# Sums of the seven-product keys read per pair of PSUM banks, and one summed form of x split early

## The chip, the cores and the metric

The kernel runs on one core of one Trainium2 chip. Its metric is the device time of one execution in microseconds (us). Before the change the median of three runs is 595.16 us (593.99 to 596.32). The engines are PE (matrix products), DVE (vector), ACT (scalar functions), POOL and SP, whose queue issues the DMAs. SBUF is the memory on the chip, PSUM the banks that PE writes its products to; DVE and ACT read them from there.

## The reference

Two stages, all in float32. Batch 8, 8 heads of 64, sequence 576, model width 512, inner width 1024.

```
p_packed = softmax(p k^T / 8) v            # 32 packed rows a head
x        = softmax(q p_packed^T / 8) p_packed
x        = heads side by side, 8 x 576 rows of 512
x_prev   = x moved by one row (zeros first)
xk = mu_k x + (1 - mu_k) x_prev ;  xr = mu_r x + (1 - mu_r) x_prev
out = sigmoid(xr w_r) * ( relu(xk w_k)^2 w_v )
```

## The kernel before

The 8 x 576 = 4608 rows of x are worked in nine blocks of 512 rows. Each block needs its gates (`xr w_r`), its keys (`xk w_k`, then relu and square), and its values (the squares times `w_v`, times the gates). Every operand of these products is held as two float32r parts, a high one and a low one, and a product is three matmuls: high by high, high by low, low by high. So one 128 x 128 by 128 x 512 product is three matmuls.

The last two blocks (`PAIR`, called first and second here) have their keys computed together. Rows and columns are taken as a 2 x 2 arrangement: the two blocks of xk by its two halves of width (a, b for the first block and c, d for the second), and `w_k` by its halves of rows and columns. Seven products instead of eight give the four results; this is Strassen's scheme in Winograd's form. `quarters` builds the row side: A11 is a, A12 is b, S3 = a - c, S2 = d - S3, S1 = a + S2, S4 = b - S2, A22 is d. `sums_of_w` builds the sums of `w_k` (T1 to T4) earlier. Each row form is split into a high and a low part on DVE (`parted_form`: a cast at L1419 and a subtraction at L1421), two row blocks u a form, and the parts lie in two tiles (`form_tiles`), one buffer each, taken from the four `xt` buffers.

`keys_of_pair` then runs the seven passes in the order A11, A12, S2, S3, S1, A22, S4. A pass goes over four column blocks j, and for each over two row blocks u, with three matmuls (L1551 to L1553), 24 in all. Four passes go into Z, four PSUM banks of one tile each (`m`, shown as `ph`): A11 leaves P1 there, S2 adds to it (U2), S3 adds again (U3), A22 again. After A11, S2 and S3, ACT copies each bank to SBUF (`kept`, L1471), and only then may the next pass add to that bank. Three passes go into X: A12, S1 and S4. X is four banks that lie in pairs in two PSUM tiles (`twin`, shown as `pa`), j = 0 and 1 in the first, 2 and 3 in the second. Behind these, `made_of` adds the bank to the copy of P1, U3 or U2 on DVE (L1484), and ACT takes relu and square in place (L1489, L1491). The results lie in SBUF tiles `q`, two column blocks a tile, in eight `sq` buffers; `home` takes two for each of the four results. A pass gives its two form buffers back when its last matmul is issued:

```
for slot, _ in forms[name]:
    flow.give("xt", slot)
```

`parted_square` splits a square into two parts for the value product (L1508, L1510). Its buffers come from `xk`, freed as the forms S3, S1, A22 and S4 are made, and from `xt`, freed after the passes. The value product of a block goes over eight blocks f of squares (L1250 to L1252), f = 0 to 3 from the first column half, 4 to 7 from the second.

The order of the work is not written out by hand. A planner (`Flow`) runs all these generators with an estimated cost for each instruction (`vec`, `act`, `pe`), picks the one that could start first by its estimate, and issues the instructions in that order; each engine then takes its own in that order. `take` and `give` hand out buffers, `wait` and `set` are events; both order the plan. The waits that the chip makes come from the tiles that the instructions read and write: who comes later in the order waits for who came earlier on the same tile.

Of the kernel before, what the change touches and what calls it, by code (L numbers as in the profile page):

```python
# [9 lines left out]
F32R = mybir.dt.float32r  # L10
# [163 lines left out]
def attn_pack_channel_mix(ctx: ExitStack, tc: tile.TileContext, q, k, v, p, mu_k, mu_r, w_k, w_v, w_r, out):  # L174
# [1200 lines left out]
    def quarters():  # L1375

        yield from mix(PAIR[0], 2, xrs, "xr")
        yield from mix(PAIR[1], 2, xrs, "xr")
        flow.now.rank = 1.1
        A, slots = {}, {}  # L1380
        for i in PAIR:
            for h in range(2):
                slots[i, h] = yield from flow.take("xk")
                A[i, h] = tile_([P, HC, TB], F32, "xk", slots[i, h], "xq")
            yield from mixed_whole(i, 0, [A[i, c // HC][:, c % HC, :] for c in range(NC)])
        (a, b), (c, d) = ((A[i, 0], A[i, 1]) for i in PAIR)
        (sa, sb_), (sc, sd) = ((slots[i, 0], slots[i, 1]) for i in PAIR)
        yield from formed("A11", a)
        yield from formed("A12", b)
        forms["S2"] = yield from form_tiles()  # L1390
        for u in range(HC):
            yield vec(TB)
            nc.vector.tensor_tensor(c[:, u, :], a[:, u, :], c[:, u, :], op=ALU.subtract)
            st_ = yield from flow.take("tmp")
            s2 = tile_([P, TB], F32, "tmp", st_, "s2")
            yield vec(TB)
            nc.vector.tensor_tensor(s2, d[:, u, :], c[:, u, :], op=ALU.subtract)
            yield from parted_form("S2", s2, u)
            yield vec(TB)
            nc.vector.tensor_tensor(a[:, u, :], a[:, u, :], s2, op=ALU.add)  # L1400
            yield vec(TB)
            nc.vector.tensor_tensor(b[:, u, :], b[:, u, :], s2, op=ALU.subtract)
            flow.give("tmp", st_)
        for name, x, slot in (("S3", c, sc), ("S1", a, sa), ("A22", d, sd), ("S4", b, sb_)):
            yield from formed(name, x)
            flow.give("xk", slot)

    def form_tiles():
        got = []
        for part in range(2):  # L1410
            slot = yield from flow.take("xt")
            o = LEAD["xt"][slot]
            got.append((slot, tile_([P, 2 * (S + 1)], F32R, "xt", slot, "form")[:, o:o + HC * TB].rearrange("p (u t) -> p u t", u=HC)))
        return got

    def parted_form(name, x, u):
        (_, h), (_, l) = forms[name]
        yield vec2(TB)
        nc.vector.tensor_copy(h[:, u, :], x)  # L1419
        yield vec(TB)  # L1420
        nc.vector.tensor_tensor(l[:, u, :], x, h[:, u, :].bitcast(F32), op=ALU.subtract)  # L1421
        flow.set((name, u))
# [24 lines left out]

    def keys_of_pair():

        ms, pas = [], []  # L1450
        for j in range(HF):
            ms.append((yield from flow.take("m")))
        Z = [ps.tile([P, TB], F32, name="ph", tag=f"m{slot}") for slot in ms]
        pas = yield from two_slots()
        twin = [banks(slot) for slot in pas]
        X = [twin[j // 2][:, j % 2, :] for j in range(HF)]
        Q = {}

        def home(i, h):
            for g in range(HF // 2):  # L1460
                slot = yield from flow.take("sq")
                Q[i, h, g] = slot, tile_([P, 2, TB], F32, "sq", slot, "q")
            flow.set(("home", i, h))

        def rest(i, h, j):
            return Q[i, h, j // 2][1][:, j % 2, :]

        def kept(n, j, i, h):
            yield from flow.wait(("home", i, h))
            yield act(TB)  # L1470
            nc.scalar.copy(rest(i, h, j), Z[j])  # L1471
            flow.set(("kept", n, j))

        def made_of(bank, j, i, h, n):
            yield from flow.wait(("home", i, h))
            to = rest(i, h, j)
            if n is None:
                yield act(TB)
                nc.scalar.activation(to, bank[j], AF.Relu)
                flow.give("m", ms[j])  # L1480
            else:
                yield from flow.wait(("kept", n, j))
                yield vec(TB)
                nc.vector.tensor_tensor(to, bank[j], to, op=ALU.add)  # L1484
                flow.set(("read", i, h, j))
                if (i, h) == (PAIR[0], 1) and j % 2:
                    flow.give("pa", pas[j // 2])
                yield act(TB)
                nc.scalar.activation(to, to, AF.Relu)  # L1489
            yield act(TB)  # L1490
            nc.scalar.activation(to, to, AF.Square)  # L1491
            flow.set(("r", i, HF * h + j))

        def squares():
            for i in PAIR:
                for f in range(NF):
                    yield from flow.wait(("r", i, f))
                    tag = "xk" if f < HF else "xt"
                    slot = yield from flow.take(tag)
                    o = LEAD[tag][slot] if tag == "xt" else 0  # L1500
                    size = 2 * (S + 1) if tag == "xt" else 2 * TB
                    hl = tile_([P, size], F32R, tag, slot, "hl")[:, o:o + 2 * TB].rearrange("p (u t) -> p u t", u=2)
                    flow.spawn(parted_square(i, f, slot, hl), 0)

        def parted_square(i, f, slot, hl):
            raw = rest(i, f // HF, f % HF)
            yield vec2(TB)
            nc.vector.tensor_copy(hl[:, 0, :], raw)  # L1508
            yield vec(TB)
            nc.vector.tensor_tensor(hl[:, 1, :], raw, hl[:, 0, :].bitcast(F32), op=ALU.subtract)  # L1510
            sqs[i, f] = slot, hl
            flow.set(("sq", i, f))

        flow.spawn(squares(), 0.5)
        first, second = PAIR
        for h in range(2):
            flow.spawn(home(first, h), 0)
            flow.spawn(home(second, 1 - h), 0)

        def own(c, o):  # L1520
            return [(wk_h[:, c + u, o:o + WP], wk_l[:, c + u, o:o + WP]) for u in range(HC)], ()

        def summed(name):
            return None, [(name, u) for u in range(HC)]

        passes = (
            ("A11", own(0, 0), Z, True, None, lambda j: kept("P1", j, first, 0)),
            ("A12", own(HC, 0), X, True, None, lambda j: made_of(X, j, first, 0, "P1")),
            ("S2", summed(T2), Z, False, "P1", lambda j: kept("U2", j, first, 1)),
            ("S3", summed(T3), Z, False, "U2", lambda j: kept("U3", j, second, 1)),  # L1530
            ("S1", summed(T1), X, True, (first, 0), lambda j: made_of(X, j, second, 1, "U3")),
            ("A22", summed(T4), Z, False, "U3", lambda j: made_of(Z, j, second, 0, None)),
            ("S4", own(HC, WP), X, False, (second, 1), lambda j: made_of(X, j, first, 1, "U2")),
        )
        for n, (name, (ws, events), bank, opens, before, evict) in enumerate(passes):
            yield from flow.wait(*events)
            if ws is None:
                ws = [small[events[u]] for u in range(HC)]
            for j in range(HF):
                if isinstance(before, str):  # L1540
                    yield from flow.wait(("kept", before, j))
                elif before:
                    yield from flow.wait(("read", *before, j))
                js = slice(j * P, (j + 1) * P)
                for u in range(HC):
                    yield from flow.wait((name, u))
                    (_, xh), (_, xl) = forms[name]
                    yield pe(0.685)
                    flow.now.t -= flow.LAG
                    wh, wl = ws[u][0][:, js], ws[u][1][:, js]  # L1550
                    nc.tensor.matmul(bank[j], wh, xh[:, u, :], start=(opens and u == 0), stop=False, skip_group_check=(not opens))  # L1551
                    nc.tensor.matmul(bank[j], wh, xl[:, u, :], start=False, stop=False, skip_group_check=(not opens))  # L1552
                    nc.tensor.matmul(bank[j], wl, xh[:, u, :], start=False, stop=(u == HC - 1), skip_group_check=(not opens))  # L1553
                flow.spawn(evict(j), 0, flow.t + flow.LAG)
            for slot, _ in forms[name]:
                flow.give("xt", slot)

    def fronts():
        for b in range(B):
# [94 lines left out]
```

## Time and profile before

| | us | share of the span |
|---|---|---|
| profiled execution | 595.77 | |
| its span, first to last instruction | 593.6 | |
| PE busy | 576.8 | 97% |
| DVE busy | 407.7 | 69% |
| ACT busy | 321.1 | 54% |
| median of three runs | 595.16 | |

The mean granted clock of TensorE over the span is 0.997 of full speed. Busy time is the time in which an engine had an instruction under way. The chain of waits follows the work back from the last instruction, and says whose work set the end. The passes of the pair run between 497.6 and 546.1 us of the span, the value products of both blocks after them.

### The profile page before, as it was taken

To read this page: it belongs to the slowest core of one execution; us is meant where nothing else is said; L and a number is where in the kernel's file an instruction comes from. 1 tells how busy PE (TensorE), PEld (TensorE's weight loads), DVE (VectorE), ACT (ScalarE), POOL (GpSimd) and SP (SyncE) were. 2 spreads that over 40 slices of the span, in tenths; PEclk is the share of its full clock that TensorE was granted. 3 is DMA by queue.
4 is the path that set the end of the run, shared out by engine and by line. 5 is a ranking of instruction groups with operands and counts; after the bars stand their busy time and mean duration, and the time that the engine had idled before them with its cause. 6 is when DMAs were issued, how large, how long until landed. Compare 5 with 4: busy or idle time off the path is not lost.

```text
span 593.6 us, 10565 instructions
## 1 busy us (share of the span) xinstructions
PE 576.8 (97%) x4091; PEld 451.6 (76%) x4091; DVE 407.7 (69%) x766; ACT 321.1 (54%) x581; POOL 7.8 (1%) x33
## 2 busy tenths in 40 slices
PE   7999999999999999999999999999999999788997
PEld 6877777687777778777877777777788888566885
DVE  1999799857792997198738877659865564766421
ACT  5679974755743682377347745547555553447000
POOL 3000000000000000000000000000000000000000
PEclk9999999999999999999999999999999999899999
DMA  8897331863466365327613755710100010000011
GB/s 301 332 258 218 106 62 20 192 135 51 111 136 142 78 114 129 85 39 142 145 72 71 155 101 152 157 25 0 72 1 0 1 72 1 0 1 1 0 72 71
DMA packets 160594, 56.67 MB, mean 95 GB/s; under 512 B 136856, under 2 KB 150304, under 8 KB 160544
## 3 DMA queue, kind: packets, MB, share of 16 engines
q1 hardware_dynamic: 160224, 55.86, 37.4%
q8 instruction: 32, 0.52, 0.4%
q0 software_dynamic: 320, 0.14, 0.1%
q14 instruction: 18, 0.15, 0.1%
HBM read 43.00 MB, written 12.98 MB: 94 GB/s over the span
## 4 chain that ended last, share of the span: by engine, by line
PE 73%; DVE 16%; DMA 4%; ACT 3%; issue 2%; SPq 1%; DVEq 0%; ACTq 0%
PE pvo L1250 8%; PE pvo L1251 8%; PE pvo L1252 8%; PE ph L1162 8%; PE ph L1163 7%; PE ph L1164 7%; PE pr L1211 5%; PE pr L1213 5%; PE pr L1212 5%; DVE x L1117 2%; PE pa L706 2%; DMA st<-in_moe_w_r 1%; PE ph L1552 1%; PE ph L1553 1%; PE ph L1551 1%
## 5 line engine op out<-in xcount | busy, mean ns | idle before, releaser
L1162 PE MATMUL ph<-xk,wk_h 128*128 128x512 f32 x224 | 90.7, 405 | 0.0
L1250 PE MATMUL pvo<-wv,sq 128*128 128x512 f32 x224 | 89.0, 397 | 0.0
L1163 PE MATMUL ph<-xk,wk_h 128*128 128x512 f32 x224 | 87.5, 391 | 0.0
L1164 PE MATMUL ph<-xk,wk_l 128*128 128x512 f32 x224 | 87.3, 390 | 0.0
L1251 PE MATMUL pvo<-wv,sq 128*128 128x512 f32 x224 | 87.3, 390 | 0.0
L1252 PE MATMUL pvo<-wv,sq 128*128 128x512 f32 x224 | 87.2, 389 | 0.0
L1174 ACT ACTIVATE r<-ph 128x512 f32<-128x512 f32 x56 | 33.6, 601 | 52.2 <-PE ph L1164 50.2
L1211 PE MATMUL pr<-wr_h,xr 128*128 128x512 f32 x144 | 57.8, 401 | 0.9 <-ACT xr L1137 0.7
L1213 PE MATMUL pr<-wr_h,xr 128*128 128x512 f32 x144 | 56.3, 391 | 0.8 <-DVE xr L1139 0.8
L1212 PE MATMUL pr<-wr_l,xr 128*128 128x512 f32 x144 | 56.2, 390 | 0.0
L1162 PEld LDWEIGHTS ph<-xk,wk_h 128*128 128x128 f32 x224 | 42.0, 188 | 14.3 <-issue 5.9
L1250 PEld LDWEIGHTS pvo<-wv,sq 128*128 128x128 f32 x224 | 42.1, 188 | 13.6 <-issue 4.9
L1117 DVE SCALAR_TENSOR_TENSOR x<-xt,mus,x 128x128 f32<-128x128 f32 (+6 forms) x100 | 46.5, 504 | 4.7 <-ACT x L1111 4.5
L1252 PEld LDWEIGHTS pvo<-wv,sq 128*128 128x128 f32 x224 | 42.0, 188 | 9.0
L1164 PEld LDWEIGHTS ph<-xk,wk_l 128*128 128x128 f32 x224 | 42.0, 188 | 9.0
L1251 PEld LDWEIGHTS pvo<-wv,sq 128*128 128x128 f32 x224 | 42.1, 188 | 8.1
L1111 ACT ACTIVATE x<-xt,mus 128x128 f32<-128x128 f32 (+6 forms) x100 | 47.6, 522 | 1.2 <-DVE sq L1187 1.2
L1163 PEld LDWEIGHTS ph<-xk,wk_h 128*128 128x128 f32 x224 | 42.1, 188 | 7.6 <-DVE xk L1056 0.2
L1185 DVE CAST sq<-r 128x512 fp32r<-128x512 f32 x48 | 20.1, 418 | 34.2 <-ACT r L1177 33.5
L1187 DVE TENSOR_TENSOR sq<-r,sq 128x512 fp32r<-128x512 f32 x56 | 38.0, 679 | 4.1 <-ACT sq L1182 3.3
L1072 ACT COPY xt<-pa 128x576 f32<-128x576 f32 x28 | 30.6, 1173 | 10.8 <-PE pa L898 10.7
L1177 ACT ACTIVATE r<-r 128x512 f32<-128x512 f32 x56 | 35.5, 634 | 1.2
(205 smaller groups left out, 977.9 us busy)
## 6 DMA issues: line engine op xcount, KB each, us to landing
vt<-in_v SPq DMA_DIRECT2D x14, 512.0 KB, 4.6
raw<-in_k SPq DMA_DIRECT2D x96, 72.0 KB, 2.7
raw<-in_q SPq DMA_DIRECT2D x96, 72.0 KB, 2.7
out<-sig SPq DMA_DIRECT2D x27, 256.0 KB, 3.0
st<-in_moe_w_k SPq DMA_DIRECT2D x8, 512.0 KB, 9.9
st<-in_moe_w_v SPq DMA_DIRECT2D x8, 512.0 KB, 4.7
far<-at SPq DMA_DIRECT2D x12, 288.0 KB, 2.5
aTd<-far SPq DMA_DIRECT2D x12, 256.0 KB, 3.0
```

Source lines behind the costliest of these rows:

```text
L1111: nc.scalar.mul(x32[:, o:o + n], xts[b, c][:, 1 + s:1 + s + n], mus[:, j, c:c + 1])
L1117: nc.vector.scalar_tensor_tensor(x32[:, o:o + n], xts[b, c][:, s:s + n], mus[:, j + 1, c:c + 1], x32[:, o:o + n], op0=ALU.mult, op1=ALU.add,)
L1162: nc.tensor.matmul(ph, wk_h[:, c, fs], xh, start=(c == 0), stop=False)
L1163: nc.tensor.matmul(ph, wk_h[:, c, fs], xl, start=False, stop=False)
L1164: nc.tensor.matmul(ph, wk_l[:, c, fs], xh, start=False, stop=(c == NC - 1))
L1187: nc.vector.tensor_tensor(hl[:, 1, :], r, hl[:, 0, :].bitcast(F32), op=ALU.subtract)
L1211: nc.tensor.matmul(pr, xh[:, ts_], wr_h[:, c, :], start=(c == 0), stop=False)
L1212: nc.tensor.matmul(pr, xh[:, ts_], wr_l[:, c, :], start=False, stop=False)
L1213: nc.tensor.matmul(pr, xl[:, ts_], wr_h[:, c, :], start=False, stop=(c == NC - 1))
L1250: nc.tensor.matmul(pv[t], sh, wvs[f][:, 0, :], start=(f == 0), stop=False)
L1251: nc.tensor.matmul(pv[t], sh, wvs[f][:, 1, :], start=False, stop=False)
L1252: nc.tensor.matmul(pv[t], sl, wvs[f][:, 0, :], start=False, stop=(f == NF - 1))
```

## The change

It does two things in the keys of the pair.

First, `made_of` is replaced by `added` and `last_of_four`. `added` does nothing after an even j. After an odd j it adds the whole pair, both banks of the tile, to the whole tile `q` in one instruction of 1024 elements, and relu and square also run over 1024. `last_of_four` is the former case of A22, which reads a Z bank alone and is as before.

Second, the tiles of the form S2 are taken from two `sq` buffers in place of two `xt` buffers. A form now carries the tag of its buffers, and they are given back to that tag behind the pass. The other six forms take `xt` buffers as before.

```diff
         yield from formed("A11", a)
         yield from formed("A12", b)
-        forms["S2"] = yield from form_tiles()
+        early = []
+        for part in range(2):
+            slot = yield from flow.take("sq")
+            early.append(("sq", slot, tile_([P, HC, TB], F32R, "sq", slot, "form")))
+        forms["S2"] = early
...
-        def made_of(bank, j, i, h, n):
-            yield from flow.wait(("home", i, h))
-            to = rest(i, h, j)
-            if n is None:
-                yield act(TB)
-                nc.scalar.activation(to, bank[j], AF.Relu)
-                flow.give("m", ms[j])
-            else:
-                yield from flow.wait(("kept", n, j))
-                yield vec(TB)
-                nc.vector.tensor_tensor(to, bank[j], to, op=ALU.add)
-                flow.set(("read", i, h, j))
-                if (i, h) == (PAIR[0], 1) and j % 2:
-                    flow.give("pa", pas[j // 2])
-                yield act(TB)
-                nc.scalar.activation(to, to, AF.Relu)
+        def last_of_four(j):
+            yield from flow.wait(("home", second, 0))
+            to = rest(second, 0, j)
+            yield act(TB)
+            nc.scalar.activation(to, Z[j], AF.Relu)
+            flow.give("m", ms[j])
             yield act(TB)
             nc.scalar.activation(to, to, AF.Square)
+            flow.set(("r", second, j))
+
+        def added(j, i, h, n):
+            if not j % 2:
+                return
+            yield from flow.wait(("home", i, h), ("kept", n, j - 1), ("kept", n, j))
+            to = Q[i, h, j // 2][1]
+            yield vec(2 * TB)
+            nc.vector.tensor_tensor(to, twin[j // 2], to, op=ALU.add)
+            flow.set(("read", i, h, j - 1))
+            flow.set(("read", i, h, j))
+            if (i, h) == (first, 1):
+                flow.give("pa", pas[j // 2])
+            yield act(2 * TB)
+            nc.scalar.activation(to, to, AF.Relu)
+            yield act(2 * TB)
+            nc.scalar.activation(to, to, AF.Square)
+            flow.set(("r", i, HF * h + j - 1))
             flow.set(("r", i, HF * h + j))
...
-            ("A12", own(HC, 0), X, True, None, lambda j: made_of(X, j, first, 0, "P1")),
+            ("A12", own(HC, 0), X, True, None, lambda j: added(j, first, 0, "P1")),
...
-            for slot, _ in forms[name]:
-                flow.give("xt", slot)
+            for tag, slot, _ in forms[name]:
+                flow.give(tag, slot)
```

## Rows read from the trace of the kernel before

**Rows 1.** The page: busy time of the engines; the chain that ended last, by engine.

```profile
PE 576.8 (97%) x4091; PEld 451.6 (76%) x4091; DVE 407.7 (69%) x766; ACT 321.1 (54%) x581; POOL 7.8 (1%) x33
...
PE 73%; DVE 16%; DMA 4%; ACT 3%; issue 2%; SPq 1%; DVEq 0%; ACTq 0%
```

**Rows 2.** Waits, 497.5 to 546.1: waiter, releaser, total us, times, longest us.

```profile
DVE form L1419 <- PE ph L1553: 9.9, 3, 6.0
...
PE pa L1551 <- DVE q L1484: 4.1, 5, 0.9
...
PE ph L1551 <- DVE form L1419: 2.4, 1, 2.4
```

**Rows 3.** Windows: stretch, length, busy PE PEld DVE ACT POOL, granted clock, DMA, GB/s.

```profile
497.58:503.02 5.44, 5.44 (x26) 4.50 (x24) 0.00 (x0) 2.36 (x4) 0.00 (x0) 1.00 0.01 3
503.02:509.60 6.58, 5.73 (x25) 4.42 (x24) 3.61 (x6) 3.12 (x5) 0.00 (x0) 1.00 0.00 0
...
514.70:517.70 3.00, 3.00 (x8) 2.34 (x7) 2.80 (x7) 0.85 (x2) 0.00 (x0) 0.50 0.00 0
...
525.32:533.05 7.73, 6.02 (x26) 4.35 (x25) 5.15 (x9) 3.92 (x7) 0.00 (x0) 1.00 0.00 1
533.05:538.50 5.45, 5.45 (x26) 4.50 (x24) 3.77 (x7) 4.60 (x9) 0.00 (x0) 1.00 0.00 0
538.50:546.09 7.59, 6.03 (x26) 4.35 (x25) 3.93 (x7) 4.75 (x9) 0.00 (x0) 1.00 0.01 2
546.09:589.80 43.71, 43.71 (x193) 35.85 (x191) 16.00 (x29) 1.73 (x3) 0.00 (x0) 1.00 0.08 29
```

**Rows 4.** Timeline of PE in A12 and S2: start, us, engine, line [idle before].

```profile
504.15 0.39 PE L1553 MATMUL pa<-form,wk_l 128*128 128x512 f32 x1
...
504.83 0.39 PE L1553 MATMUL pa<-form,wk_l 128*128 128x512 f32 x1
506.07 0.50 PE L1551 MATMUL pa<-form,wk_h 128*128 128x512 f32 x1 [0.85 <-DVE q L1484]
...
507.56 0.39 PE L1551 MATMUL pa<-form,wk_h 128*128 128x512 f32 x1
...
510.06 0.39 PE L1553 MATMUL ph<-form,T 128*128 128x512 f32 x1
512.88 0.49 PE L1551 MATMUL ph<-form,T 128*128 128x512 f32 x1 [2.43 <-DVE form L1419]
```

**Rows 5.** Timeline of DVE, 495 to 513 us.

```profile
495.78 0.68 DVE L1393 TENSOR_TENSOR xq<-xq 128x512 f32<-128x512 f32 x1
...
503.22 0.43 DVE L1419 CAST form<-s 128x512 fp32r<-128x512 f32 x1 [6.02 <-PE ph L1553]
505.32 0.69 DVE L1484 TENSOR_TENSOR q<-pa,q 128x512 f32<-128x512 f32 x1 [1.68 <-PE pa L1553]
...
507.14 0.69 DVE L1484 TENSOR_TENSOR q<-pa,q 128x512 f32<-128x512 f32 x1 [0.53 <-PE pa L1553]
...
509.87 0.69 DVE L1484 TENSOR_TENSOR q<-pa,q 128x512 f32<-128x512 f32 x1 [0.84 <-PE pa L1553]
...
512.86 0.69 DVE L1421 TENSOR_TENSOR form<-s,form 128x512 fp32r<-128x512 f32 x1
```

**Rows 6.** Groups by line: tile, out<-in, count, busy us, mean ns, idle before.

```profile
L1484 DVE TENSOR_TENSOR q<-pa,q 128x512 f32<-128x512 f32 x12 | 8.3, 690 | 9.5 <-PE pa L1553 8.6 <-ACT q L1491 0.8
...
L1489 ACT ACTIVATE q<-q 128x512 f32<-128x512 f32 x12 | 7.6, 632 | 11.7 <-DVE q L1484 11.7
L1471 ACT COPY q<-ph 128x512 f32<-128x512 f32 x12 | 7.0, 587 | 11.4 <-PE ph L1553 11.4
...
L738 ACT COPY ppT<-pa 128x128 f32<-128x128 f32 x7 | 1.9, 265 | 11.2 <-PE pa L735 11.2
...
L996 DVE TENSOR_TENSOR pms<-pm,mub 128x128 f32<-128x128 f32 x2 | 0.6, 284 | 0.0
```

**Rows 7.** Timeline of ACT: the last gate of the pair's first block.

```profile
486.90 0.60 ACT L1231 ACTIVATE sig<-pr 128x512 f32<-128x512 f32 x1 [1.28 <-PE pr L1213]
```

More of the change, by code (lines that the diff above doesn't have):

```diff
@@ L1412, in form_tiles @@
             o = LEAD["xt"][slot]
-            got.append((slot, tile_([P, 2 * (S + 1)], F32R, "xt", slot, "form")[:, o:o + HC * TB].rearrange("p (u t) -> p u t", u=HC)))
+            got.append(("xt", slot, tile_([P, 2 * (S + 1)], F32R, "xt", slot, "form")[:, o:o + HC * TB].rearrange("p (u t) -> p u t", u=HC)))
         return got
     def parted_form(name, x, u):
-        (_, h), (_, l) = forms[name]
+        (*_, h), (*_, l) = forms[name]
         yield vec2(TB)
@@ L1448, in keys_of_pair @@
     def keys_of_pair():
+        first, second = PAIR
         ms, pas = [], []
@@ L1514, in keys_of_pair @@
         flow.spawn(squares(), 0.5)
-        first, second = PAIR
         for h in range(2):
@@ L1527, in keys_of_pair @@
             ("A11", own(0, 0), Z, True, None, lambda j: kept("P1", j, first, 0)),
-            ("A12", own(HC, 0), X, True, None, lambda j: made_of(X, j, first, 0, "P1")),
+            ("A12", own(HC, 0), X, True, None, lambda j: added(j, first, 0, "P1")),
             ("S2", summed(T2), Z, False, "P1", lambda j: kept("U2", j, first, 1)),
             ("S3", summed(T3), Z, False, "U2", lambda j: kept("U3", j, second, 1)),
-            ("S1", summed(T1), X, True, (first, 0), lambda j: made_of(X, j, second, 1, "U3")),
-            ("A22", summed(T4), Z, False, "U3", lambda j: made_of(Z, j, second, 0, None)),
-            ("S4", own(HC, WP), X, False, (second, 1), lambda j: made_of(X, j, first, 1, "U2")),
+            ("S1", summed(T1), X, True, (first, 0), lambda j: added(j, second, 1, "U3")),
+            ("A22", summed(T4), Z, False, "U3", lambda j: last_of_four(j)),
+            ("S4", own(HC, WP), X, False, (second, 1), lambda j: added(j, first, 1, "U2")),
         )
@@ L1546, in keys_of_pair @@
                     yield from flow.wait((name, u))
-                    (_, xh), (_, xl) = forms[name]
+                    (*_, xh), (*_, xl) = forms[name]
                     yield pe(0.685)
```

## The prediction

> **What bounds the kernel now.** Read the page's first and fourth parts first [rows 1]: PE is busy for 97% of the span and carries 73% of the chain that ended last; DVE carries 16%. So PE's stream is the length of the kernel, and a change can only shorten it where PE pauses or runs slowly. The waits of the stretch that the change touches come next [rows 2]: PE waits five times for the sum `q` of L1484 and once for the form of L1419, and DVE's own queue had stood up to 6.0 us before that form, waiting for PE's L1553. The windows by pass then give the price [rows 3]. One pass is 4 column blocks x 2 row blocks x 3 matmuls = 24 matmuls. The pass A11 runs without a pause, 497.58 to 503.02, 5.44 us, or 0.227 us a matmul. So seven passes at that pace take 38.08 us; they take 48.51 (497.58 to 546.09), 10.43 too many. Pass by pass: A12 6.58 (1.14 over), S2 and S3 together 15.72 (509.60 to 525.32; 4.84 over), S1 7.73 (2.29 over), A22 5.45, S4 7.59 (2.15 over). Behind them PE is busy for all 43.71 us of the two value products, so nothing waits there, and what the passes save arrives at the end whole.
>
> **What makes the three passes of the paired banks wait.** Their results lie two to a PSUM tile (`twin`), and the kernel sums each half by itself. In A12 the last matmul of j=0 started at 504.15, but its sum started only at 505.32, after j=1's matmul of 504.83 had finished; and PE's next matmul, also of j=1, started at 506.07, after that sum [rows 4, 5]. The two banks differ, the tile is one: the order is kept by tile. A matmul that comes behind the sum in the program's order waits for it although it writes the other half. The five waits cost 1.14 + 2.29 + 2.15 = 5.58 us, 1.1 each. (A12 has only one: DVE came to the sum of j=2 at 509.87, when PE had already issued all of that pair.)
>
> **What makes S2 late.** Its two form tiles are taken from the `xt` buffers, and A11 and A12 hold all four. DVE had computed s2 by 497.2 and then stood 6.02 us until 503.22, when A11's last matmul freed the first pair [rows 5]. After that its queue mixes the rest of S2 with sums that wait for PE; the second row block's low part starts at 512.86, its high part just before, and PE stands from 510.06 to 512.88 [rows 4, 5]. Right behind this pause the granted clock is 0.50, that is 1.2 GHz, from 514.70 to 517.70 [rows 3]: some 3.0 us at half pace, with its edges about 3.2, of which half, 1.6, is lost. So the 4.84 is 3.2 of pause and first matmuls and 1.6 of clock.
>
> **The change, part by part.**
>
> Sums by pair. Twelve sums of 512 become six of 1024. DVE took 690 ns for 512 and 284 for 128 (L996) [rows 6], 1.06 ns an element, so 1024 is estimated at 690 + 512 x 1.06 = 1.23 us. Bounds: 0.69 (no dearer than now) and 1.38 (two of now); I take 1.23. For ACT 587 at 512 and 265 at 128 give 0.84 ns an element, so relu and square are 632 + 430 = 1.06 each (bounds 0.63 and 1.26). DVE's work falls from 12 x 0.69 = 8.3 to 7.4, ACT's from 24 x 0.63 = 15.2 to 12.7; neither is on the path. What counts is that no matmul of a pair lies behind that pair's sum any more, as the sum is issued after j odd. The next matmuls write the other tile. That this does not wait shows in A12: the sum of j=1 reads the first pair from 507.14 to 507.83, while PE goes on with j=2 on the second, at 507.56 without a pause [rows 4, 5]. Gain 5.58; bounds 0 and 5.58.
>
> What becomes later: the sum of j even, by one block, 1.36 us. Behind it hang the next write of the bank and the squares. S1 writes A12's banks two passes later, S4 writes S1's one pass later: the sum of S1's first pair ends at about 523.5 in the new times below, S4 opens at 530.2. The squares of S4 are first read at the fifth block of the value product, 4 x 12 x 0.227 = 10.9 us after S4; sum, relu, square, cast and low part of the last pair need 1.23 + 1.06 + 1.06 + 2 x 1.12 = 5.6. Hidden.
>
> S2 in two `sq` buffers. Block 7's gates ended at 486.90 (its last sigmoid, [rows 7]) and freed four; DVE needs two at 497.2. So DVE runs on: 2 x (4 x 0.68 + 0.43 + 0.69) = 7.7 us from 495.78, all of S2 ready by 503.5 [rows 5]. S2 then opens at 503.02 + 5.44 = 508.46, 5 us later. The four homes of the results want eight `sq` buffers and find six; the fourth is for A22's result and waits until S2's end, 513.9, while its first writer comes at 526. Nothing.
>
> What is late next. All later forms need 2 x 1.12 = 2.2 us of DVE and get their buffers from the pass two or more ahead. S3: A11's pair at 503.2, ready 505.7, wanted 513.9. S1: A12's pair at 508.7, behind it one pair sum and two squares at worst, ready 514.5, wanted 519.3. A22: S3's pair at 519.5, ready 521.8, wanted 524.8. S4: S1's pair at 525.0, one pair sum in front, ready 528.4, wanted 530.2. Smallest lead 1.8 us. On ACT, S3's first matmul wants S2's first copy by 513.9; with relu and square of a pair in front it is done at about 510.1 + 2.1 + 0.6 = 512.8, 1.1 to spare. The clock: without the pause nothing in the passes lowers it, so the 1.6 comes back too.
>
> Sum: 5.58 + 4.84 = 10.4. The value product opens at 535.7 instead of 546.09. The profiled execution took 595.77 around a span of 593.6: 585.4 after. It stands 0.6 above the median of the runs, 595.16, so that the median comes to **584.8**.
>
> One rule speaks for less. The clock fell behind one long pause and not behind the five short ones [rows 3, 4]. The Trainium skill ("TensorE: Matmul & The Clock Gate", "What's actually happening") says that the moment at which the chip changes this clock is not tied to the kernel and differs between runs of the same one. By it some runs of before never paid the 1.6, the gain would be 8.8 in these and the median up to 586.4. No run here shows such a one.
>
> **The rivals.**
>
> 1. Part of the leads don't hold: a form or a copy comes late once or twice, or one pair still waits. For it: 1.1 and 1.8 us are thin, and DVE and ACT take their queues in order, as the 6.0 us stand shows [rows 2]. Against: the queue's busy work leaves room (between 519 and 530 two forms, two pair sums and two squares, 4.5 + 2.5 + 2.2 = 9.2 of 11 us). Two waits of 1.1 give 587; the case that S2's pause merely moves to the next pass leaves 5.58 of gain, 589.6.
>
> 2. The change doesn't do what it says: the wait is not of the tile but of every earlier sum, so that each pair sum stops the next matmul. A wait costs 1.14 with a sum of 0.69, so 1.68 with 1.23; six make 10.1, against 10.43 gained: no change, 594.8. Against it stands the overlap at 507.56.
>
> 3. Slower: in DVE's queue the forms of S1, A22 and S4 land behind pair sums that themselves wait for PE, as S2's second row block does now. Price of one such lateness with its spell of low clock: 4.84 [rows 3]. Three make 14.5, 4.1 more than is gained: 599.2. It decides from a form that gets over 3.2 us (5.44 - 2.2) of other work in front on DVE, three times. For it: the order is planned with estimated times. Against: a pair sum is 1.23.
>
> **How the numbers follow.** The forecast has 0.80, with its own range 583.4 (a run as low as the lowest of before, 1.2 under the median, and the full gain) to 586.6 (no clock in it). Rival 1 has 0.14, spread over 586.6 to 591; rival 2 has 0.03; rival 3 has 0.03. To leave out no more than 2 in 10 the range goes some way into rival 1: 583.3 to 588.2. The unknown costs (pair sum, relu, square) are hidden at either bound. 0.5% is 3.0 us, about what a measurement can tell from no change: faster 0.94 (forecast and rival 1), same 0.03, slower 0.03.
>
> **What would show it.** Six sums of 128x1024 of about 1.23 us and no wait of PE for them; the form of S2 begun at about 497 on DVE without a stand; granted clock 1.00 in all seven passes, each 5.44 us; L1250's first matmul of these blocks at about 535.7; DVE and ACT otherwise unchanged. It is wrong if a pass is over 5.6 us long; which engine ended that wait then names the lead that failed.

## The result, and the profile after

The changed kernel takes 585.34 us in the median of five runs (584.78 to 585.79), against 595.33 for the kernel before: a ratio of 0.9833, 95% interval 0.9817 to 0.9849, or 10.0 us less. Forecast were 584.8 (583.3 to 588.2) and 10.4 less.

The windows by pass of the kernel after, cut at the first matmul of each pass (columns as in [rows 3]; the third row is S2 and S3 together, the last one the value products):

```profile
496.94:502.38 5.44, 5.44 (x26) 4.51 (x24) 5.23 (x10) 2.37 (x4) 0.00 (x0) 1.00 0.01 3
502.38:507.82 5.44, 5.44 (x26) 4.51 (x24) 3.71 (x6) 1.75 (x3) 0.00 (x0) 1.00 0.00 0
507.82:518.70 10.88, 10.88 (x50) 9.01 (x48) 5.25 (x9) 6.76 (x10) 0.00 (x0) 1.00 0.00 0
518.70:524.14 5.44, 5.44 (x26) 4.51 (x24) 4.40 (x7) 1.19 (x2) 0.00 (x0) 1.00 0.00 0
524.14:529.58 5.44, 5.44 (x26) 4.51 (x24) 4.31 (x7) 5.41 (x9) 0.00 (x0) 1.00 0.02 3
529.58:535.02 5.44, 5.44 (x26) 4.51 (x24) 1.23 (x1) 3.49 (x7) 0.00 (x0) 1.00 0.00 0
535.02:578.73 43.71, 43.68 (x193) 35.86 (x191) 17.89 (x32) 3.01 (x3) 0.00 (x0) 1.00 0.08 29
```

All seven passes run at 5.44 us with PE busy throughout and the granted clock at 1.00: 38.08 us in all, 10.43 less than before. The value products take the same 43.71, and nothing is given back behind them. The profiled execution is 11.0 us shorter than that of before, since its A11 also began 0.64 earlier (496.94 against 497.58). The code ahead of A11 does the same work, and that start moves between profiled executions anyway: 496.72 to 498.70 over the experiments below. So the passes are compared by their own length, and times by medians.

The timeline of DVE after, where [rows 5] had a stand of 6.02 us and sums of 512:

```profile
496.66 0.43 DVE L1423 CAST form<-s 128x512 fp32r<-128x512 f32 x1
...
500.91 0.69 DVE L1425 TENSOR_TENSOR form<-s,form 128x512 fp32r<-128x512 f32 x1
...
505.37 1.23 DVE L1495 TENSOR_TENSOR q<-pa,q 128x1024 f32<-128x1024 f32 x1 [0.44 <-PE pa L1565]
...
508.36 1.22 DVE L1495 TENSOR_TENSOR q<-pa,q 128x1024 f32<-128x1024 f32 x1
...
526.87 0.69 DVE L1425 TENSOR_TENSOR form<-xq,form 128x512 fp32r<-128x512 f32 x1
```

S2 is split from 496.66 on, without a stand, and its last part is done at 501.6, 6.2 us before the pass that reads it. The last row is S4's form: done at 527.56, and S4 opens at 529.58, a lead of 2.0.

The groups by line after, to set beside [rows 6]:

```profile
L1495 DVE TENSOR_TENSOR q<-pa,q 128x1024 f32<-128x1024 f32 x6 | 7.3, 1221 | 5.7 <-PE pa L1565 5.7
...
L1503 ACT ACTIVATE q<-q 128x1024 f32<-128x1024 f32 x6 | 6.4, 1062 | 0.1
L1501 ACT ACTIVATE q<-q 128x1024 f32<-128x1024 f32 x6 | 6.4, 1060 | 10.0 <-DVE q L1495 10.0
```

### The profile page after: what moved, and what is told of

Read it like the earlier page. It is cut to its first block, busy times and chain, and to the rows that moved or that the text cites. A ratio compares the mean times of both kernels' runs of the same rounds, so it can differ in the third digit from the quotient of the medians.

```text
span 582.5 us, 10546 instructions
## 1 busy us (share of the span) xinstructions
PE 573.4 (98%) x4091; PEld 452.0 (78%) x4091; DVE 406.3 (70%) x760; ACT 317.6 (55%) x569; POOL 7.8 (1%) x33
## 4 chain that ended last, share of the span: by engine, by line
PE 81%; DVE 11%; DMA 3%; ACT 3%; issue 1%; SPq 1%; DVEq 0%; ACTq 0%
PE pvo L1250 9%; PE pvo L1252 9%; PE pvo L1251 9%; PE ph L1162 8%; PE ph L1163 8%; PE ph L1164 8%; PE pr L1211 6%; PE pr L1213 5%; PE pr L1212 5%; PE pa L706 2%; DMA st<-in_moe_w_r 2%; DVE x L1117 1%; PE pa L898 1%; PE ph L1564 1%; PE ph L1565 1%; PE ph L1563 1%
```

## The experiments

Each is compared with runs of the kernel before on the same chip (median 595.35 us for e1 to e4, 595.37 for e5 to e8, which ran on another chip). "Passes" is the stretch from A11's first matmul to that of the value products, in the profiled execution; its length without a pause is 38.08.

| kernel | median us (runs) | ratio to before, 95% interval | passes us |
|---|---|---|---|
| before, profiled | | | 48.51 |
| e1, pair sums alone | 588.01 (587.50 to 589.16) | 0.9881 [0.9862, 0.9900] | 40.68 |
| e2, early S2 alone | 591.78 (591.24 to 593.22) | 0.9950 [0.9935, 0.9965] | 44.83 |
| e3, halves behind the pair | 584.87 (584.79 to 585.24) | 0.9832 [0.9817, 0.9848] | 38.08 |
| e4, before again | 595.72 (594.30 to 596.75) | 1.0008 [0.9998, 1.0018] | 48.54 |
| e5, S2 late | 592.06 (591.39 to 592.70) | 0.9942 [0.9925, 0.9959] | 44.11 |
| e6, sums twice as dear | 585.56 (584.96 to 585.81) | 0.9832 [0.9814, 0.9850] | 38.08 |
| e7, sums three times as dear | 586.43 (585.62 to 587.15) | 0.9848 [0.9829, 0.9867] | 39.26 |
| e8, after again | 585.16 (584.96 to 585.47) | 0.9828 [0.9810, 0.9845] | 38.08 |

**e1, the pair sums alone.** The changed kernel with S2's buffers as they were:

```diff
-        early = []
-        for part in range(2):
-            slot = yield from flow.take("sq")
-            early.append(("sq", slot, tile_([P, HC, TB], F32R, "sq", slot, "form")))
-        forms["S2"] = early
+        forms["S2"] = yield from form_tiles()
```

> The sums by pair alone; S2 takes its forms from the xt buffers as before. Theory (the two parts each remove a wait of their own): the five waits of 1.1 us of PE for the sums are gone, S2 is still late. In the planned order the second row block of S2 now stands on DVE behind the second pair sum of A12, so PE should pause once in S2, from about 509 to 511.5, with a spell of half clock behind it: 3 to 5 us of the 10.43 stay, 588.0 to 590.0 us; strictly additive parts give 595.3 - 5.6 = 589.7. Rival (S2 was late only because the single sums held DVE up, so the buffers don't matter): no pause in S2, 585.3 as with both parts.

The waits of PE in the passes of e1, all there are (columns as in [rows 2]), PE's row behind the first of them, and DVE's timeline around them:

```profile
PE ph L1559 <- DVE form L1419: 1.8, 1, 1.8
PE ph L1560 <- DVE form L1421: 0.2, 1, 0.2
```

```profile
512.19 0.49 PE L1559 MATMUL ph<-form,T 128*128 128x512 f32 x1 [1.77 <-DVE form L1419]
```

```profile
504.34 0.43 DVE L1419 CAST form<-s 128x512 fp32r<-128x512 f32 x1 [6.02 <-PE ph L1561]
...
509.85 1.22 DVE L1491 TENSOR_TENSOR q<-pa,q 128x1024 f32<-128x1024 f32 x1 [0.30 <-PE pa L1561]
...
511.71 0.43 DVE L1419 CAST form<-s 128x512 fp32r<-128x512 f32 x1
```

The waits for sums are gone. DVE still stands 6.02 us for A11's buffers, and S2's second row block lands behind the second pair sum, as the order said: its cast is 7.4 us behind that of the first. PE pauses once, and the passes are 2.60 too long, in place of 10.43. But the mean clock is 1.00 in all four runs, so that the time came out at the lower edge of what was expected, and the strictly additive 589.7 is above every run. The rival (no pause without the single sums) falls too.

**e2, the early S2 alone.** The kernel before, with S2 in `sq` buffers as in the change and `made_of` kept:

```diff
-        forms["S2"] = yield from form_tiles()
+        early = []
+        for part in range(2):
+            slot = yield from flow.take("sq")
+            early.append(("sq", slot, tile_([P, HC, TB], F32R, "sq", slot, "form")))
+        forms["S2"] = early
...
```

The rest of the edit gives each form the tag of its buffers, as in the change.

> The early S2 alone; the sums read one bank each as before. Theory: the pause in S2 and its spell of half clock are gone, 4.84, but the sums' waits stay, and since DVE is no longer behind, the second pair of A12 gets its wait too: six waits of 1.14 in place of five, so 6.8 of the 10.43 stay: 591.7. Strictly additive parts would leave five: 590.5. Rival (the waits of the sums come from a DVE that is late): no waits, 585.3.

The waits of PE in the passes of e2, and two rows of PE's timeline in A12:

```profile
PE pa L1555 <- DVE q L1488: 4.9, 6, 0.9
```

```profile
505.30 0.50 PE L1555 MATMUL pa<-form,wk_h 128*128 128x512 f32 x1 [0.85 <-DVE q L1488]
...
509.10 0.50 PE L1555 MATMUL pa<-form,wk_h 128*128 128x512 f32 x1 [0.79 <-DVE q L1488]
```

Six waits, the new one in A12's second pair at 509.10. They take 44.83 - 38.08 = 6.75 us, 1.13 each, and the median is 591.78 where 591.7 was expected. A DVE that is not late makes more of these waits, not fewer. So they are not waits for a busy DVE.

**e3, sums of 512 again, but behind the pair.** S2 is early as in the change; sums, relu and square are of 512 each as before, and only their place in the order is that of the change:

```diff
-            to = Q[i, h, j // 2][1]
-            yield vec(2 * TB)
-            nc.vector.tensor_tensor(to, twin[j // 2], to, op=ALU.add)
...
+            flow.spawn(half(j - 1, i, h), 0)
+            flow.spawn(half(j, i, h), 0)
+
+        def half(j, i, h):
+            to = rest(i, h, j)
+            yield vec(TB)
+            nc.vector.tensor_tensor(to, X[j], to, op=ALU.add)
...
```

> Both parts, but the sums are again twelve of 512, one bank each; they are only issued behind the second half's matmuls, where the pair sum stands. Theory (what matters is that no matmul of a tile stands behind a read of that tile in the order): no wait of PE in the passes, 585.3 as with the pair sums, within 0.5. Rival (what matters is the width, one instruction in place of two, or DVE's and ACT's smaller work): the waits come back at least in part, 588 to 592.

The passes of e3 in one window, and its sums:

```profile
497.07:535.15 38.08, 38.08 (x169) 31.53 (x168) 25.06 (x46) 22.38 (x40) 0.00 (x0) 1.00 0.01 1
```

```profile
L1499 DVE TENSOR_TENSOR q<-pa,q 128x512 f32<-128x512 f32 x12 | 7.7, 683 | 4.1 <-PE pa L1567 4.1
```

No pause with twelve sums of 512. The single wide instruction is not what frees PE; that no matmul of a tile follows, in the same pass, a read of that tile in the order is. Its 584.87 and the 585.34 and 585.16 of the change (the last from e8) lie too close for this to be called a faster version.

**e4, the kernel before once more**, unchanged.

> The kernel before once more, for the granted clock of each run. Theory: the pause of S2 is followed by half clock in every run, so each run's mean clock is at 0.997 or below and the spread of the times is not the 1.6 us of that spell. Rival (the clock falls in some runs only): runs at 0.999 or 1.000 among them, and these 1.6 us faster.

In its own twelve runs the theory holds: each has 0.996 or 0.997. Over more runs the rival does. With the runs of before from both comparisons there are 40 with a granted clock each: 34 with a mean of 0.996 or 0.997 and a median of 595.6 us (594.30 to 596.75), six with 0.998 to 1.000 and 593.9 (593.48 to 594.94). The difference, 1.6 to 1.7 us, is the size that the prediction gave the half-clock spell. So it is paid in most executions and, by the mean clock, not in every one; of the six no trace was kept, and the one with 0.998 may have paid a part.

**e5, one pause in S2 and no other.** The change, with S2's second row block held back:

```diff
         for u in range(HC):
+            if u:
+                yield from flow.wait(("read", PAIR[0], 0, HF - 1))
+                yield vec(2 * TB)
+                nc.vector.tensor_reduce(
+                    const.tile([P, 1], F32, name="mx", tag="mx0"), parts["twin"][1], axis=AX.XY, op=ALU.max)
             yield vec(TB)
...
```

The rest of the edit makes the two tiles of X known here, as `parts["twin"]`.

> The changed kernel, but the second row block of S2 is held on DVE until the second pair sum of A12 and one extra reduction of that pair (its result is not used) are done. Expected is one pause of PE in S2 of about 3.6 us and none elsewhere. Theory (a pause as long as the one of the kernel before or longer is followed by the spell of half clock, whatever the sums do): 3.8 of pause and first matmuls and 1.6 of clock, 585.3 + 5.4 = 590.7, mean clock 0.996 or 0.997 in most runs. Rival (the spell came from the pause together with the short waits around it): clock 1.000, 589.1.

PE's timeline of e5 at the pause (its two waits are all that PE has in the passes), and the window of the spell behind it:

```profile
513.56 0.49 PE L1568 MATMUL ph<-form,T 128*128 128x512 f32 x1 [3.63 <-DVE form L1428]
514.29 0.50 PE L1569 MATMUL ph<-form,T 128*128 128x512 f32 x1 [0.23 <-DVE form L1430]
```

```profile
514.95:517.93 2.98, 2.98 (x8) 2.31 (x7) 2.91 (x7) 0.77 (x2) 0.00 (x0) 0.50 0.00 0
```

One pause of the expected 3.6 us, no short waits around it, and behind it the same spell at 1.2 GHz. All six runs have a mean clock of 0.994 to 0.997; the rival's 1.000 does not occur. So the short waits are not needed behind a pause of this length; it is longer than the 2.43 us of the kernel before, so that what a pause of 2.43 alone would do is not shown. The passes are 6.03 too long where 5.4 was expected: the first pause alone is 3.78 (513.56 less the matmul before at 509.55 and its 0.23), and the second wait and the slow first matmuls add the 0.6 that was left out. The median, 592.06, is 6.9 above e8, 0.9 more than the passes explain, and that stays open; two of the runs have a mean clock of 0.994, lower than the profiled one's 0.997, and of these there is no trace.

**e6, pair sums twice as dear.** One reduction of the pair ahead of each sum (e7 has two):

```diff
+            for _ in range(1):
+                yield vec(2 * TB)
+                nc.vector.tensor_reduce(
+                    const.tile([P, 1], F32, name="mx", tag="mx0"), twin[j // 2], axis=AX.XY, op=ALU.max)
             yield vec(2 * TB)
             nc.vector.tensor_tensor(to, twin[j // 2], to, op=ALU.add)
```

> The changed kernel with one extra reduction of 1024 elements (result not used) ahead of each of the six pair sums, so that a sum costs DVE twice as much, about 2.4 us. Theory (the sum lies beside PE, the smallest lead is S4's forms with 2.0 us): S4's forms end some 1.5 us later, still in time: no wait of PE over 0.3 us, 585.3 to 585.7. Rival (leads are used up already, rival 1 of the prediction): S4 or S3 waits over 0.5 us, 586 to 588.

The passes of e6 in one window, and its extra reductions:

```profile
498.05:536.13 38.08, 38.08 (x169) 31.53 (x168) 29.59 (x44) 19.73 (x30) 0.00 (x0) 1.00 0.00 1
```

```profile
L1496 DVE TENSOR_REDUCE mx<-pa 128x1 f32<-128x1024 f32 x6 | 7.3, 1220 | 3.1 <-PE pa L1569 3.1
```

7.3 us more on DVE, and not one pause.

**e7, three times as dear.**

> The same with two extra reductions ahead of each sum, about 3.6 us a sum. Theory: S4's forms end about 3 us later than in the changed kernel, over their lead of 2.0: one pause of 0.5 to 1.5 us at the opening of S4 and none elsewhere, 586.0 to 587.0. Rival (queue order: forms land behind sums that wait for PE, three times over, rival 3 of the prediction): pauses in S1, A22 and S4, above 590.

PE's timeline of e7 at the opening of S4, and DVE's:

```profile
530.25 0.50 PE L1568 MATMUL pa<-form,wk_h 128*128 128x512 f32 x1 [0.51 <-DVE form L1425]
...
531.32 0.50 PE L1568 MATMUL pa<-form,wk_h 128*128 128x512 f32 x1
```

```profile
528.38 1.22 DVE L1499 TENSOR_TENSOR q<-pa,q 128x1024 f32<-128x1024 f32 x1
529.52 0.68 DVE L1425 TENSOR_TENSOR form<-xq,form 128x512 fp32r<-128x512 f32 x1
...
530.57 0.69 DVE L1425 TENSOR_TENSOR form<-xq,form 128x512 fp32r<-128x512 f32 x1
```

Here the leads end, and at the form that was named: S4's low part starts at 529.52, S4 waits for it, and the passes are 1.18 too long (39.26). The low part of the second row block ends at 531.26, and the matmul that reads it starts at 531.32, a quarter of a microsecond late: so the one pause that was expected is two, both at S4's forms. Nothing else waits.

**e8, the changed kernel once more**, unchanged.

> The changed kernel once more, beside the others on one chip. Theory: 585.3, clock 0.999 or 1.000 in every run. If the twelve sums of 512 behind the pair (584.87) are truly faster than the six of 1024, this stays 0.4 above them; if that was noise, it comes out at 585 +- 0.5.

585.16, clock 0.999 or 1.000 in each run: the same time again, and 10.2 below the runs of before beside it. Against e3, which ran on the other chip, the ratios to before are what can be compared: 0.9828 here and 0.9832 there, with intervals that overlap, so no difference between six wide sums and twelve narrow ones is shown.

## Why the prediction was right

**The place of the sum.** Right, and the cause is shown from three sides: the change has no wait, e3 has none with the old width in the new place, e2 keeps them all and gains a sixth. Rival 2 (each pair sum stops the next matmul) would have left the time as it was. That it is the shared tile which makes the order, and not the neighbouring bank, is argued from overlaps: no run gives the four banks of X a tile each. The four banks of Z have one each, and there PE did not wait. In A11 of the kernel before it went on in the second bank while ACT read the first:

```profile
499.16 0.39 PE L1552 MATMUL ph<-form,wk_h 128*128 128x512 f32 x1
```

```profile
499.14 0.59 ACT L1471 COPY q<-ph 128x512 f32<-128x512 f32 x1 [0.76 <-PE ph L1553]
```

**The cost of the sums.** 1.23 forecast, 1.22 to 1.23 measured; relu and square 1.06 forecast, 1.06 measured. That they are hidden at either bound held far beyond it: at twice the cost (e6) nothing shows in the passes.

**S2 early.** Right: forecast ready by 503.5, with an opening at 508.46, 5 us of lead; after, 501.6 and 507.82, 6.2. The count of `sq` buffers held: no copy to a home came late.

**What is late next.** S4's lead was forecast as 1.8 and is 2.0. The other thin one, S2's first copy on ACT, was forecast with 1.1 to spare, with relu and square of a pair in front. The planner put it ahead of both. This is its row in ACT's timeline after:

```profile
509.38 0.59 ACT L1476 COPY q<-ph 128x512 f32<-128x512 f32 x1 [0.60 <-PE ph L1565]
```

It is done at 509.97, and S3 opens at 507.82 + 5.44 = 513.26: 3.3 to spare. Rival 1 (part of the leads don't hold) needed DVE's sums at three times their cost before it came true, in e7, and then for 1.18 us. Rival 3, three such lapses, stayed far off. DVE still waits for buffers after the change, 5.53 us ahead of A22's form:

```profile
518.90 0.43 DVE L1423 CAST form<-xq 128x512 fp32r<-128x512 f32 x1 [5.53 <-PE ph L1565]
```

It costs nothing, as that form is done at 521.11 and A22 opens at 524.14, with the forecast lead of 3.0. A long wait in DVE's queue is no loss by itself; the lead behind it decides.

**The clock.** The 1.6 for the spell was right in size (e4's 40 runs). That it follows the pause is shown in part: e5 has the spell behind one pause of 3.63 us and no short waits, and e2 has six short waits and no spell. The pause of the kernel before was 2.43, e1's of 1.77 had no spell behind it, and whether the 2.43 would have been enough without the short wait in A12 ahead of it stays open. The sentence that the 1.6 comes back was too simple in one point: six runs of before show little or nothing of the spell. The rule of the Trainium skill ("TensorE: Matmul & The Clock Gate", "What's actually happening") is that the moment of the change differs between runs of one kernel. The runs agree with it as far as they go: in the two traces of before the granted clock is 0.50 from 514.5 and, in e4, from about 514.6, some 1.6 and 1.7 us after PE had gone on (512.88 and 512.92), and whether the spell comes at all differs too. The median gained the 1.6 all the same, since 34 of 40 paid.

**The two terms.** 5.58 + 4.84, with the 0.01 of A22 10.43, was right as a sum for both parts together; as the worth of either part alone the terms are wrong, which the prediction did not say. In the passes the pair sums alone save 48.51 - 40.68 = 7.83, the early S2 alone 48.51 - 44.83 = 3.68. The pair sums shorten S2's pause as well (from 2.43 to 1.77 at the first matmul) and spare the clock; and S2, once early, lets one more sum come in time to stop PE. Whoever had tried the second part alone would have found a third of the gain.

**The range.** Its inner lower end, 583.4, does not follow from its own terms: 584.8 less 1.2 is 583.6. Nothing hangs on it, as no run of the result was under 584.78.

## What to carry to other kernels

Where two PSUM banks are one tile, look in the profile for a matmul that waits for a read of the other half. Each such wait cost 1.13 us here, of which the read itself is 0.69, and all went when the read was issued behind the tile's last matmul, in one instruction or in two. Where a queue that takes its work in order waits for a buffer, look whether another tag has one free: two `sq` buffers ended a wait of 6.02 us. The savings of two waits that share a queue don't add: price each part alone only with the other wait still in place.

## What the runs showed of the hardware

Which pauses were followed by the lower clock: in e1 PE paused 1.77 us and 0.23 again, and the mean clock was 1.00 in all four runs, so there was none. In the kernel before it paused 2.43 and 0.23 in both traces, with a short wait of 0.85 in A12 ahead of these, and 34 of 40 runs show the lower clock; the profiled one spent 3.0 us and its edges at 1.2 GHz. In e5 it paused 3.63 and 0.23, and all six runs show the lower clock. How long a pause must be is not shown. The six short waits of e2, 0.85 us at most, left the mean at 0.999 or 1.000 in all six runs.

One vector instruction read two PSUM banks, 1024 elements, in 1.22 us, 0.16 less than two reads of 512 at 0.69; the reduction over the same two banks took 1.22 as well.
